# Key/query stores and weight loads in one order on SyncE in the first batched stage, and the third round's output weights behind the keys in the chain's first segment

## The chip, the cores and the metric

The kernel runs on one core of a Trainium2 chip. The metric is device time in microseconds (us) of one execution; a measurement is the median of several. A core has TensorE (PE in the profile; PEld is its weight loads), VectorE (DVE), ScalarE (ACT), GpSimd (POOL) and SyncE (SP). SyncE only issues transfers. ACT and POOL compute and issue transfers too, and each engine works through its own instructions in order, so an ACT instruction that waits to issue a transfer holds back all ACT work behind it. The transfers themselves are done by 16 DMA engines that all queues share.

## The reference

There are four layers, A B A B, on x of 2048 rows and 640 columns in bfloat16. The change touches the A layers only, a memory-augmented recurrent attention:

```python
for s in range(n_seg):                      # 64 segments of 32 rows
    h = concatenate([mem, xs])              # 8 memory rows + 32 rows of x (normalised)
    q, k, v = h @ Wq, h @ Wk, h @ Wv        # 640 -> 32 heads of 192
    p = softmax(mask(q @ k.T * scale))      # memory rows see all, others the past
    o = (p @ v) @ Wo                        # 6144 -> 640
    mem = o[:8]; outs.append(o[8:])
```

Segment s needs the memory rows that segment s-1 made, so the segments form a chain. A layer B (a linear attention with softmax features) follows each layer A and is the same in both kernels.

## The kernel before

**Two parts of a layer A.** Keys, queries and values of a row of x do not depend on the memory. The kernel uses this for the last 8 rows of every segment: a *batched stage* (`A_pre`) computes their keys, queries and values for all 64 segments ahead, as large matmuls, and stores them to DRAM (`kqb_d` for keys and queries, `vb_d` for values). The *chain* (`A_chain`) then goes segment by segment with the 8 memory rows and the first 24 rows, and fetches the stored 8 rows' keys, queries and values as it goes.

**Rounds.** The 32 heads are done in four rounds of 8. A round has 1536 columns of each of Wq, Wk and Wv, each in five pieces of 128 partitions by 1536 columns (384 KB), so a round has 15 pieces. In on-chip memory (one tile, `arena`) most pieces stay for the whole layer. The last three of the five pieces of each matrix are *slots* shared by rounds 0 and 3: they are loaded again whenever the other round is next (`load_slot`, L620). Pieces that stay are loaded by `load_matrix` (L626).

**The first batched stage** (layer 0, `x_raw` given) goes through eight *turns*: rounds 3, 2, 1, 0, and in each round two halves h of the segments. A turn does the keys and queries (12 column blocks each, L818, two blocks per PSUM bank) and then the values (L835). Each full PSUM bank is evicted alternately by DVE (L87) and ACT (L89); there are eight banks. After each eviction one step of a list of *tasks* runs: these normalise x row block by row block (load of `ln_x` by POOL, moments on DVE, deviation on ACT, store of `xn` by POOL). Keys and queries of a turn are gathered in one of two buffers `st`, which lie in the area that later holds the output weights of rounds 1 and 2 (`wo_mid`), and one transfer of 1536 KB stores them (L824). That store is issued by ACT. Values are stored by POOL (L843). All weight pieces of a turn are issued by SyncE where the turn begins in the program; as SyncE waits for no computation there, except before a slot is refilled, it runs ahead.

**Output weights.** Wo is used in rounds as well. Rounds 1 and 2 have areas of their own (`wo_mid`), rounds 0 and 3 share one (`wo_end`) and are read from a copy in DRAM, `wo_rows`, that `lay_out_wo` makes once, from DRAM to DRAM. `early_wo` loads the eight parts (320 KB each) whose place is free before the stage ends, `late_wo` the others, at the start of the chain.

**The chain's first segment** works in the order: queries and keys of round 0, its values, then rounds 1 to 3, each with its scores, its weighting and its share of the output (`wo_round`, L996). When round 0's slot pieces have been used they are refilled for round 3 (L620): queries, then keys, then values. The order of issue on SyncE is the order of the program text; the four late parts of the output weights of round 2 (`late_wo(2)`) stand between the refill of the queries' slots and that of the keys'.

**Semaphores of transfers.** The compiled program gives the transfers of SyncE and ACT together eight semaphores in turn. A transfer waits, before it is issued, until the transfer that last had its semaphore has landed.

The batched stage of layer 2 (no `x_raw`) keeps its stores on ACT; for the order of its SyncE instructions the same program text holds.

Of the kernel before, what the change touches and what calls it, by code (L numbers as in the profile page):

```python
# [8 lines left out]
P = 128  # L9
BF16 = mybir.dt.bfloat16  # L10
# [105 lines left out]
class Kernel:  # L116
# [465 lines left out]
    def layer_A(self, xn_dram, at_dram, li, x_raw=None):  # L582
        nc, tc = self.nc, self.tc
        KC, NSEG = self.KC, self.NSEG
        dram = self.dram
        NR = 4
        PW = 1536
        self.kqb_d = dram.tile([NSEG, P, NR, 192], BF16, name=f"kqb{li}")
        self.vb_d = dram.tile([NSEG, NR, 2, 8, 896], BF16, name=f"vb{li}")
        self.otb_d = dram.tile([NSEG, P, 384], BF16, name=f"otb{li}")  # L590
        wview = self.wview
        wov = self.A_Wo.rearrange("h d m -> (h d) m").rearrange("(c p) m -> p c m", p=P)
        low = self.view(0, LATE)
        at = LATE
        res, slot = {}, {}
        for r in (3, 2):
            for m in "KQV":
                for b in range(KC - (SLOTS[m] if r == 3 else 0)):
                    res[m, r, b] = low[:, len(res) * PW:len(res) * PW + PW]
        assert len(res) * PW * 2 == LATE  # L600
        for m, r, b in [(m, 0, b) for m in "KQV" for b in range(KC - SLOTS[m])] + \
                [(m, None, b) for m in "KQV" for b in range(KC - SLOTS[m], KC)] + [(m, 1, b) for m in "KQV" for b in range(KC)]:
            v = self.view(at, 2 * PW)
            at += 2 * PW
            if r is None:
                slot[m, b] = v
            else:
                res[m, r, b] = v
        holds = {}
        wo_mid = self.view(at, 24 * 1280)  # L610
        wo_end = self.view(at + 24 * 1280, 12 * 1280)
        assert at + 36 * 1280 == ARENA
        unread = set(res)

        def load_slot(m, r, b, whole=False):
            if holds.get((m, b)) != r:
                holds[m, b] = r
                w = PW if whole or m in "QV" else PW // 2
                for h in range(0, PW, w):
                    nc.sync.dma_start(out=slot[m, b][:, h:h + w], in_=wview[m][:, b, PW * r + h:PW * r + h + w])  # L620

        def load_matrix(m, r):
            for b in range(KC):
                if (m, r, b) in unread:
                    unread.remove((m, r, b))
                    nc.sync.dma_start(out=res[m, r, b], in_=wview[m][:, b, PW * r:PW * r + PW])  # L626
                elif (m, r, b) not in res:
                    load_slot(m, r, b, True)

        early = {(0, 4), (0, 5), (2, 4), (2, 5), (1, 0), (1, 1), (1, 2), (1, 3)}  # L630

        def load_wo(r, into=None, part=range(6)):
            t = into if into is not None else wo_end[:, :] if r in (0, 3) else wo_mid[:, 7680 * (r - 1):7680 * r]
            for k in part:
                tk = t[:, 1280 * k:1280 * k + 1280]
                if r in (0, 3):
                    self.last_load = nc.sync.dma_start(out=tk, in_=self.wo_rows[r // 3, :, 1280 * k:1280 * k + 1280])
                else:
                    nc.sync.dma_start(out=tk.rearrange("p (c m) -> p c m", m=640),
                                      in_=wov[:, 12 * r + 2 * k:12 * r + 2 * k + 2, :])  # L640

        def piece(m, r, b):
            assert (m, r, b) in res or holds[m, b] == r
            return res[m, r, b] if (m, r, b) in res else slot[m, b]

        def lay_out_wo():
            if li == 0:
                self.wo_rows = dram.tile([2, P, 7680], BF16, name="wo_rows")
                for i, r in enumerate((0, 3)):
                    (nc.sync if x_raw is not None else nc.scalar).dma_start(out=self.wo_rows[i].rearrange("p (c m) -> p c m", m=640),  # L650
                                        in_=wov[:, 12 * r:12 * r + 12, :])

        def early_wo():
            for r in (2, 0, 1):
                load_wo(r, part=[k for k in range(6) if (r, k) in early])

        def late_wo(r, part=range(6)):
            load_wo(r, part=[k for k in part if (r, k) not in early])

        self.A_pre(xn_dram, li, load_matrix, piece, wo_mid, wo_end, lay_out_wo, early_wo, x_raw)  # L660
        self.A_chain(xn_dram, at_dram, li, load_slot, piece, load_wo, late_wo, wo_mid, wo_end, low)
        self.post_args = at_dram, wo_mid, wo_end, low
# [6 lines left out]
    def A_pre(self, xn_dram, li, load_matrix, piece, wo_mid, wo_end, lay_out_wo, early_wo, x_raw):  # L669


        nc, tc, ev, KC, NSEG = self.nc, self.tc, self.ev, self.KC, self.NSEG
        NR = 4
        SH = min(NSEG, 32)
# [3 lines left out]
        NH = NSEG // SH  # L678
# [3 lines left out]
        with ExitStack() as es:  # L682
# [73 lines left out]
            def all_rows():  # L756
                rows = [slice(P * b, P * b + P) for b in range(self.NB)]
                t = in_turn([norm_tasks(lambda x, q=q: nc.gpsimd.dma_start(out=x[:], in_=x_raw[q, :]),
                                        lambda xn, q=q: nc.gpsimd.dma_start(out=xn_dram[q, :], in_=xn[:]))
                             for q in rows])  # L760
                return [f for i in range(0, len(t), 2) for f in (*t[i:i + 2], None)]
# [23 lines left out]
            for h, ri, r in steps:  # L785
# [10 lines left out]
                        if x_raw is not None:  # L796
                            busy(3)
                xBT = columns(h)
                if (h, ri) == ((NH - 1, 0) if x_raw is None else (NH - 1, 2)):
                    lay_out_wo()  # L800
                st = sts[turn % 2]
                turn += 1
                if x_raw is not None and h == 0 and ri == 1:
# [3 lines left out]
                        tasks += tails(h1)  # L807
                if x_raw is not None and (h, ri) == (NH - 1, 0):
                    tasks += all_rows()
                for mi, m in enumerate("KQ"):  # L810
                    load_matrix(m, r)
                    w = [piece(m, r, b) for b in range(KC)]
                    for c0 in range(0, 12, CB):
                        ps = ps_.tile([P, 512], F32, name="ps_pre", tag="bank")
                        for i in range(CB):
                            c = c0 + i
                            for b in range(KC):
                                nc.tensor.matmul(ps[:, T * i:T * i + T], lhsT=w[b][:, P * c:P * c + P], rhs=xBT[:, b, :],  # L818
                                                 start=(b == 0), stop=(b == KC - 1))
                        G, xi = c0 // 6, c0 % 6  # L820
                        so = st[:, :, 96 * mi:96 * mi + 96].rearrange("p s (i g t) -> p i g s t", g=2, t=8)
                        evict(out=so[:, xi:xi + CB, G],
                              in_=ps[:, :].rearrange("p (i t s) -> p i s t", i=CB, t=8))
                nc.scalar.dma_start(out=self.kqb_d[SH * h:SH * h + SH, :, r, :].rearrange("s p f -> p s f"), in_=st)  # L824
                load_matrix("V", r)
                if h == NH - 1 and ri == NR - 1:
                    early_wo()
                w = [piece("V", r, b) for b in range(KC)]
                for k in range(NT):
                    vt = vts[nv % 2]  # L830
# [18 lines left out]
    def A_chain(self, xn_dram, at_dram, li, load_slot, piece, load_wo, late_wo, wo_mid, wo_end, low):  # L849
        nc, tc, KC, NSEG = self.nc, self.tc, self.KC, self.NSEG  # L850
        scale = float(self.Dh) ** -0.5
        NR = 4
        with tc.tile_pool(name=f"A{li}_ch", reuse_waits="tile", bufs=1) as sp, \
# [79 lines left out]
            def to_rows(raw, m):  # L933
                if m == "K":
                    nc.vector.transpose(out=KT[:, :, 0:64], in_=raw[:, :].rearrange("p (c j) -> p c j", j=64))  # L935
                else:
                    rv = raw[:, :].rearrange("p (x i j) -> p x i j", i=3, j=64)
                    nc.vector.transpose(out=QT[:, :, 0:4:3, 0:64], in_=rv[:, :, 0:3:2, :])  # L938
                    nc.vector.transpose(out=QT[0:64, :, 1, 0:64], in_=rv[0:64, :, 1, :])
                    nc.vector.transpose(out=QT[64:P, :, 2, 0:64], in_=rv[64:P, :, 1, :])  # L940
# [109 lines left out]
            for s in range(NSEG):  # L1050
# [4 lines left out]
                def q_or_k(m, n):  # L1055
                    ps = pqp.tile([P, 512], F32, name="ps_qk", tag="qk")
                    project(hT, ps, m, n, s, range(KC))
                    return to_raw(ps, "OT" if m == "K" and n == 0 else "raw")
# [9 lines left out]

                to_rows(q_or_k("Q", 0), "Q")
                if s == 0:  # L1070
                    late_wo(2)
                    fill(FILL[li])
                to_rows(q_or_k("K", 0), "K")
                if s > 0:
                    store_rows(s - 1)
                pv = v_banks()
# [136 lines left out]
```

## Time and profile before

| | us |
|---|---|
| median of 3 runs | 3757.66 (3756.19 to 3761.43) |
| span of the profiled execution | 3763.4 |
| PE busy | 3553.2 (94%) |
| DVE busy | 2370.4 (63%) |
| ACT busy | 2074.7 (55%) |
| POOL busy | 1656.0 (44%) |
| first batched stage, first to last of its matmuls | 10.0 to 195.0 |
| first chain segment of layer 0 | 195.0 to 230.3 |
| second chain segment of layer 0 | 230.3 to 252.0 |
| first chain segment of layer 2 | 2065.1 to 2101.6 |

The transfers move 931.72 MB in the whole span. The stores of keys and queries are 1536 KB each, 16 in the two A layers, and take 8.9 us from issue to landing in the median, from 7.5 to 21.7. How to read it: busy time of an engine says little about what bounds a stage, because shares are averages over stages. Read the stretch of time in question, look for idle PE in it, and follow what ended each idle time.

### The profile page before, as it was taken

The page shows a single profiled execution, that of the slowest core. Times are in us where ns is not written, and L with a number is a line of the kernel's source. Part 1 is how long each engine was busy: PE and PEld are TensorE (multiplying, and loading weights), DVE is VectorE, ACT ScalarE, POOL GpSimd, SP SyncE. Part 2 cuts the span into 40 slices and gives each one's busy share as a digit, 9 for nine tenths or more (in the row PEclk, how much of TensorE's full clock was granted, in tenths as well). Part 3 has the DMA queues.
Part 4 walks back from the last instruction along what each step waited for, and adds up shares of the span by engine and source line. Part 5 has one row for each costly group of instructions (what it writes and reads, how often), then busy time and mean ns, then how long its engine had stood idle before and what let it go on. Part 6 is the DMA issues. An engine that isn't in the chain of part 4 may idle for free.

```text
span 3763.4 us, 169092 instructions
## 1 busy us (share of the span) xinstructions
PE 3553.2 (94%) x71082; PEld 2321.8 (62%) x71390; DVE 2370.4 (63%) x6330; ACT 2074.7 (55%) x5285; POOL 1656.0 (44%) x4323
## 2 busy tenths in 40 slices
PE   7989999999999999989899999999999999999898
PEld 5756666666666666555367566666666666665553
DVE  4556666666666666546633566666666666664565
ACT  2356566666666666546432556666666666665453
POOL 2445455555555555430342445555555555553400
PEclk9999999999999999989899999999999999999899
DMA  9788788888887878830387878888887888879100
GB/s 342 231 282 290 262 285 291 277 288 275 287 288 270 291 279 284 305 111 1 134 261 201 292 270 292 276 293 285 286 283 273 287 285 281 294 267 317 57 1 29
DMA packets 531381, 931.72 MB, mean 248 GB/s; under 512 B 141034, under 2 KB 298362, under 8 KB 530618
## 3 DMA queue, kind: packets, MB, share of 16 engines
q1 hardware_dynamic: 395898, 806.29, 60.9%
q0 software_dynamic: 68160, 88.78, 8.1%
q10 hardware_dynamic: 66560, 25.82, 2.7%
q8 instruction: 558, 9.14, 1.0%
q14 instruction: 205, 1.68, 0.1%
HBM read 852.43 MB, written 72.09 MB: 246 GB/s over the span
## 4 chain that ended last, share of the span: by engine, by line
PE 62%; DMA 13%; DVE 8%; ACT 6%; issue 5%; POOL 3%; PEld 2%; SPq 1%; POOLq 0%; ACTq 0%; DVEq 0%
PE ps_qk L920 19%; PE ps_w L996 8%; PE ps_v L920 8%; DMA arena<-wo_rows 6%; PE ps_o L970 4%; PE ps_s L962 4%; PE ps_pre L818 3%; PE ps_s L1028 2%; DVE hT L876 2%; PE ps_s L957 2%; DMA Vp<-vb 2%; PE ps_idle L1003 2%; PE ps_qk L389 2%; PE ps_pre L835 2%; DVE E L1035 1%
## 5 line engine op out<-in xcount | busy, mean ns | idle before, releaser
L920 PE MATMUL ps_qk<-arena,hT 128*32 128x384 bf16 x20480 | 999.1, 327 | 19.9 <-DMA arena<-in_A_Wk_dram 9.0
L920 PEld LDWEIGHTS <-hT 128*32 128x32 bf16 x30720 | 738.0, 96 | 437.0 <-DVE hT L1139 28.9
L930 ACT ACTIVATE raw<-ps_qk 128x384 bf16<-128x384 f32 x1024 | 502.9, 491 | 390.2 <-PE ps_s L1028 245.7
L996 PE MATMUL ps_w<-arena,OT 128*32 128x160 bf16 x24576 | 545.0, 235 | 36.8 <-issue 23.6
L903 POOL DMA_DIRECT2D Vp<-vb x512 | 258.8, 505 | 671.8 <-PE ps_o L970 462.6
L920 PE MATMUL ps_v<-arena,hT 128*32 128x384 bf16 x10240 | 537.2, 330 | 0.0
L996 PEld LDWEIGHTS <-OT 128*32 128x32 bf16 x24576 | 436.7, 97 | 132.2 <-issue 54.8
L935 DVE STREAM_TRANSPOSE KT<-raw 128x384 bf16<-128x384 bf16 x512 | 296.0, 578 | 205.7 <-ACT raw L930 201.7
L938 DVE STREAM_TRANSPOSE QT<-raw 128x256 bf16<-128x256 bf16 x512 | 227.9, 445 | 238.5 <-ACT raw L930 196.4
L891 POOL DMA_DIRECT2D kqb<-kqb x512 | 291.1, 568 | 163.0 <-POOL KT L899 148.2
L951 DVE CAST Vp<-ps_v 64x384 bf16<-64x384 f32 x512 | 286.0, 559 | 89.4 <-ACT Vp L949 75.8
L989 POOL DMA_DIRECT2D otb<-otb x512 | 282.8, 552 | 118.1 <-DVE otb L985 100.5
L949 ACT ACTIVATE Vp<-ps_v 64x384 bf16<-64x384 f32 x512 | 246.3, 481 | 149.6 <-PE ps_v L920 108.2
L976 DVE CAST OT<-ps_o 128x192 bf16<-128x192 f32 x512 | 183.2, 358 | 221.2 <-PE ps_o L970 203.2
L1035 DVE TENSOR_TENSOR E<-E,ps_s 80x320 bf16<-80x320 bf16 x512 | 247.4, 483 | 73.7 <-ACT ps_s L1034 69.7
L1014 ACT ACTIVATE E<-ps_s 80x320 bf16<-80x320 f32 x512 | 221.9, 433 | 127.7 <-PE ps_s L962 99.3
L970 PEld LDWEIGHTS <-Vp 80*128 80x128 bf16 x4096 | 183.8, 99 | 160.5 <-issue 124.8
L970 PE MATMUL ps_o<-E,Vp 80*128 80x80 bf16 x4096 | 234.2, 202 | 26.7 <-DVE E L1035 7.5
L962 PE MATMUL ps_s<-QT,KT 128*80 128x80 bf16 (+1 forms) x3072 | 233.7, 213 | 22.3 <-DVE KT L935 11.7
L975 ACT ACTIVATE OT<-ps_o 128x192 bf16<-128x192 f32 x512 | 167.8, 328 | 148.3 <-PE ps_o L970 147.1
L884 ACT ACTIVATE Vp<-ps_w 32x160 bf16<-32x160 f32 x512 | 150.7, 294 | 177.1 <-DVE wt L1138 151.5
L962 PEld LDWEIGHTS <-KT 128*80 128x80 bf16 x3072 | 195.6, 119 | 70.9 <-issue 59.8
(152 smaller groups left out, 5471.9 us busy)
## 6 DMA issues: line engine op xcount, KB each, us to landing
arena<-wo_rows SPq DMA_DIRECT2D x792, 320.0 KB, 6.9
arena<-in_A_Wq_dram SPq DMA_DIRECT2D x427, 384.0 KB, 4.6
arena<-in_A_Wv_dram SPq DMA_DIRECT2D x427, 384.0 KB, 6.3
arena<-in_A_Wk_dram SPq DMA_DIRECT2D x768, 192.0 KB, 4.8
kqb<-arena ACTq DMA_DIRECT2D x16, 1536.0 KB, 8.9
kqb<-kqb POOLq DMA_DIRECT2D x512, 48.0 KB, 5.1
arena<-in_A_Wk_dram SPq DMA_DIRECT2D x43, 384.0 KB, 6.4
vb<-arena POOLq DMA_DIRECT2D x128, 112.0 KB, 5.7
```

Source lines behind the costliest of these rows:

```text
L891: nc.gpsimd.dma_start(out=kqb[:], in_=self.kqb_d[s, :, r, :])
L903: nc.gpsimd.dma_start(out=Vs[n % 2][64:80, :], in_=self.vb_d[s, r].rearrange("g t f -> (g t) f"))
L920: nc.tensor.matmul(o[32 * g:32 * g + 32, 0:384], lhsT=hT[:, b, :], rhs=rhs, start=(i == 0), stop=(i == KC - 1), tile_position=(0, 32 * g), ...
L930: nc.scalar.activation(out=raw[:], in_=ps[:, 0:384], func=ACT.Copy)
L935: nc.vector.transpose(out=KT[:, :, 0:64], in_=raw[:, :].rearrange("p (c j) -> p c j", j=64))
L949: nc.scalar.activation(out=o, in_=i, func=ACT.Copy)
L951: nc.vector.tensor_copy(out=o, in_=i)
L962: nc.tensor.matmul(S[0:80, c0:c0 + 80 * (q1 - q0)], lhsT=KT[:, 3 * x + i, :], rhs=QT[:, x, q0:q1, :], start=False, stop=(x == 1 and i == 2 ...
L970: nc.tensor.matmul(O[x][:, 80 * i:80 * i + 80], lhsT=Vs[n % 2][0:80, 448 * x + k:448 * x + k + 128], rhs=E[0:80, 160 * x + 80 * e:160 * x ...
L989: nc.gpsimd.dma_start(out=self.otb_d[s, :, 96 * r:96 * r + 96], in_=otb[:, :, :].rearrange("p c t -> p (c t)"))
L996: nc.tensor.matmul(W[32 * g:32 * g + 32, 0:160], lhsT=OT[:, c, q:q + 32], rhs=w[:, 640 * i + 160 * g:640 * i + 160 * g + 160], start=(firs ...
L1035: nc.vector.tensor_tensor(out=E[0:80, 0:320], in0=E[0:80, 0:320], in1=rc, op=ALU.mult)
```

## The change

In the first batched stage the stores of keys and queries move from ACT to SyncE, into one order with the weight loads: a turn's store stands behind the round's values, and in the first half of a round the next round's 15 weight pieces follow the store directly. Before, the weights of a round were issued with no regard to stores. `lay_out_wo` now makes one of the two copies at a time, behind the stores of the second half of the rounds two and three, instead of both ahead of the second half of round three. `early_wo` is called ahead of the last turn's keys, where it was behind that turn's last weights. In the chain, `late_wo(2)` moves from ahead of the refill of the keys' slots to behind it; this holds for both A layers. The purpose is that no compute engine waits to issue a store, and that loads arrive in the order in which they are needed.

```diff
-        def lay_out_wo():
-            if li == 0:
-                self.wo_rows = dram.tile([2, P, 7680], BF16, name="wo_rows")
-                for i, r in enumerate((0, 3)):
-                    (nc.sync if x_raw is not None else nc.scalar).dma_start(out=self.wo_rows[i].rearrange("p (c m) -> p c m", m=640),
-                                        in_=wov[:, 12 * r:12 * r + 12, :])
+        if li == 0:
+            self.wo_rows = dram.tile([2, P, 7680], BF16, name="wo_rows")
+
+        def lay_out_wo(i):
+            nc.sync.dma_start(out=self.wo_rows[i].rearrange("p (c m) -> p c m", m=640), in_=wov[:, 36 * i:36 * i + 12, :])
...
-                if (h, ri) == ((NH - 1, 0) if x_raw is None else (NH - 1, 2)):
-                    lay_out_wo()
...
+                if x_raw is not None and h == NH - 1 and ri == NR - 1:
+                    early_wo()
                 for mi, m in enumerate("KQ"):
                     load_matrix(m, r)
...
-                nc.scalar.dma_start(out=self.kqb_d[SH * h:SH * h + SH, :, r, :].rearrange("s p f -> p s f"), in_=st)
                 load_matrix("V", r)
-                if h == NH - 1 and ri == NR - 1:
+                if x_raw is None and h == NH - 1 and ri == NR - 1:
                     early_wo()
+                stq = nc.scalar if x_raw is None else nc.sync
+                stq.dma_start(out=self.kqb_d[SH * h:SH * h + SH, :, r, :].rearrange("s p f -> p s f"), in_=st)
+                if x_raw is not None:
+                    if h == 0 and ri + 1 < NR:
+                        for m in "KQV":
+                            load_matrix(m, NR - 2 - ri)
+                    if h == NH - 1 and ri in (1, 2):
+                        lay_out_wo(ri - 1)
...
                 to_rows(q_or_k("Q", 0), "Q")
                 if s == 0:
-                    late_wo(2)
                     fill(FILL[li])
                 to_rows(q_or_k("K", 0), "K")
+                if s == 0:
+                    late_wo(2)
```

## The prediction

> **What bounds the kernel now.** I read busy time by stretch first, then the instructions in order of time, then who waited for whom. The first batched stage runs from 11.2 to 195.0 us. In stretches of 25 us (columns: length; PE, PEld, DVE, ACT, POOL busy with counts; granted clock; DMA share; GB/s):
>
> ```profile
> 25.00:50.00 25.00, 25.00 (x202) 19.16 (x200) 14.72 (x41) 7.78 (x18) 7.55 (x14) 1.00 0.98 333
> 50.00:75.00 25.00, 17.81 (x141) 14.24 (x139) 9.47 (x29) 6.12 (x16) 8.97 (x29) 0.86 1.02 378
> 75.00:100.00 25.00, 15.09 (x111) 11.36 (x109) 8.04 (x24) 4.08 (x11) 5.45 (x10) 0.86 0.99 329
> 100.00:125.00 25.00, 20.40 (x157) 15.46 (x154) 13.66 (x40) 6.16 (x18) 9.78 (x18) 0.93 1.02 335
> 125.00:150.00 25.00, 25.00 (x210) 20.26 (x208) 17.67 (x50) 9.61 (x22) 8.75 (x16) 1.00 0.58 168
> 150.00:175.00 25.00, 25.00 (x195) 18.92 (x194) 11.97 (x27) 7.41 (x15) 9.70 (x18) 1.00 0.61 162
> ```
>
> PE has holes from 50 to 125 us, while the DMA engines are full; from 125 on PE is full and the DMA engines are 40% empty. The holes, from PE in order of time (start, length, what, idle before and its releaser):
>
> ```profile
> 62.25 10.32 PE L818 MATMUL ps_pre<-arena 128*128 128x256 bf16 x80 [7.19 <-ACT arena L89]
> 81.68 2.34 PE L818 MATMUL ps_pre<-arena 128*128 128x256 bf16 x20 [1.52 <-DVE arena L87]
> 92.41 11.68 PE L818 MATMUL ps_pre<-arena 128*128 128x256 bf16 x90 [8.39 <-ACT arena L89]
> 110.31 6.33 PE L835 MATMUL ps_pre<-arena 128*128 128x384 bf16 x30 [4.60 <-DVE arena L87]
> ```
>
> PE waits for PSUM evictions, which stand still because ACT waits. What ACT waits for is in the waits (total us, times, longest):
>
> ```profile
> ACT arena L89 <- DMA arena<-in_A_Wk_dram: 17.3, 1, 17.3
> ACT arena L89 <- DMA arena<-in_A_Wq_dram: 14.7, 1, 14.7
> ```
>
> And in those of SyncE's queue (total, times, longest):
>
> ```profile
> SPq L626 <- DMA kqb<-arena: 26.4, 2, 14.4
> ```
>
> An eviction needs no weights. The instruction ahead of it on ACT is the store of L824: it issues at 61.12 and 91.30 us, just as those waits end. The built instruction lists say why: all DMAs of SyncE and ACT share eight semaphores in turn, so each waits until the one eight places before has landed. The second store's semaphore was last used by a query weight piece of round 1, the third's by a key piece of round 0, both weights wanted only later; SyncE in turn waits for the first store. The chain of work names the same path (start, length):
>
> ```profile
> 26.35 20.37 DMA kqb<-arena
> ...
> 52.52 8.51 DMA arena<-in_A_Wq_dram
> ...
> 79.55 11.65 DMA arena<-in_A_Wk_dram
> ...
> 96.17 11.94 DMA ln_x<-in_A_x_dram
> ```
>
> Then the chain's first segment: 195.0 to 230.3, 35.3 us, while the next takes 21.7 (230.31 to 251.97). PE waits there for late loads; layer 2 shows the same (2065.1 to 2101.6, 36.5 us):
>
> ```profile
> PE ps_qk L920 <- DMA arena<-in_A_Wk_dram: 4.2, 3, 2.8
> PE ps_w L996 <- DMA arena<-wo_rows: 2.8, 2, 1.6
> PE ps_qk L920 <- DMA arena<-in_A_Wq_dram: 1.0, 2, 0.9
> ```
>
> **What the Trainium skill says.** "DMA: Bandwidth & Descriptors", section "Issuing engines are not separate DMA queues": transfers from all queues run on the same 16 DMA engines. So moving stores from ACT to SyncE buys no bandwidth; it removes ACT's wait. The trace agrees: in stretches of 5 us with a share near 1.0 the sum is 280 to 400 GB/s whoever issues. Its "Queues, rings and completion order" says each DMA engine takes turns between queues; that fits a store that takes 20.37 us to land behind weights but 7.5 at best. "TensorE: Matmul & The Clock Gate", Part 1: an idle TensorE falls to half clock and needs some microseconds to return. The trace agrees: the granted clock is 0.50 at 60 to 65 and at 90 to 95 us.
>
> **The change, part by part.**
>
> *Stores to SyncE, weights one round ahead.* A turn of PE takes 19.6 us unhindered (136.08 to 155.68). Eight from 11.2, with 0.6 for the transposes in the first, end at 168.6 instead of 195.0: 26.4 us less. It is the four holes (21.7) plus slow matmuls behind three of them: 80 took 10.32 us and 90 took 11.68 where 120 take 13.1 elsewhere (+1.6 and +1.8), and 30 took 6.33 where 40 take 6.5 (+1.4). ACT also loses 8 issues of 0.37 us, at no gain, since it idles between evictions.
>
> The added wait: on SyncE a store waits for its turn's last evictions, and the next round's weights are queued behind it. First use against landing decides. DMA time by shares of the first 235 us: ACT's store queue 21.5%, so 6.3 us a store; weights 46.6% for 40.06 MB, so 16.1 us for a round of 5.9 MB (15 pieces of 384 KB), 5.4 for a copy of output weights (1920 KB), 7.2 for the eight early output pieces; POOL's queue 18.7% for 13.5 MB, so 3.0 a turn of value stores and 1.1 for each of 16 x rows in and out. In the new order:
> store 0 is ready at 26.4 (SyncE idles some 5 us first); store 0, round 2, values and five x rows end near 57, the first third of the weights near 42 (needed 50.5). Store 1 and values: 66. Store 2 is ready at 63.6; it and round 1, with values and x rows: 100, keys near 82 (needed 89.7), values needed 102.8. Store 3, first copy, store 4: 118. Round 0: 141 to 144, keys near 127 (needed 128.9), values needed 142. Store 5: 150, and its buffer is wanted again at 151. Second copy, store 6, early pieces: 172. Store 7: 178, values: 181.
> So every deadline holds, but from 118 on by 0 to 3 us only, and the stage ends with a DMA backlog: PE is done at 168.6, the last store lands some 10 us later; before it landed at 197.4, 2.4 after PE. The chain's output pieces wait for this store's buffer, and all slot weights are queued behind them. They come 5 to 8 us later against PE than before. I take 6 given back; both ends: 0 (my shares count time in which queues overlap; sums exceed 1.0) and 14 (V of round 0, store 5 and the chain each late by 3 to 8).
>
> *Early output pieces ahead of the last keys; copies moved.* Same loads, same order among themselves, waiting for buffers as before; their cost is in the sum above, and PE hides it. Zero.
>
> *Chain: round 2's output pieces behind the keys.* Four pieces of 320 KB leave the path of the six key pieces. At 377 GB/s (2080 to 2090) that is 3.5 us. In layer 2 the key waits sum to 4.7 and the values, whose place in the queue is unchanged, would land 1.18 MB behind the old last key (2090.2): 2091.3 to 2093.3, against use at 2090.3 onward after the shift. So about 3 of 3.5 remain. The moved pieces are used 5 us later still (2096.36): hidden. Ends: 1 (values then wait) and 5 (less slow clock, which was 0.52 from 2090 to 2100). I take 3 in each layer; in layer 0 it partly pays the backlog.
>
> *Sum:* 26.4 - 6 + 3 + 3 = 26.4 us; 3757.7 - 26.4 = 3731.
>
> **Rivals.**
> *PE alone bounds the stage:* nothing given back, and the chain gains 4 each: 3757.7 - 34.4 = 3723. For it: before moved weights up to 45 us earlier than needed, and, summed over stretches of 5 us, 32 us of DMA time lay idle up to 225. Against: those 32 us are just about what it would use up.
> *The DMA engines become the bound:* values of round 0 and store 5 are late, DVE waits for x rows (30.5 us before, longest 9.9) go on, and the chain starts on a backlog: 14 given back, no gain in layer 0's chain: 3757.7 - 26.4 + 14 - 2 = 3743; up to 3748. For it: the margins of 0 to 3 us. Against: with ACT's ring silent, x rows share the engines with one queue less.
> *Head of line, slower:* stores on SyncE take 20.4 us as store 0 did before, 14 more than assumed. One stands ahead of the keys of each later round, whose margins are 8, 8 and 2 us: 6 + 6 + 12 late; store 5, with 1 us of margin, adds 13: 37 lost against 26.4 won: 3768. Against: the 20.4 were spent sharing with weights that now stand behind the store.
>
> **How the numbers follow.** Forecast 0.50, PE alone 0.20, DMA bound 0.24, head of line 0.06. Range 3719 (chain ends at their best, 4 us under the second case) to 3748. Of the DMA-bound case a tenth falls within 0.2% (7.5 us). Faster 0.92, same 0.03, slower 0.05.
>
> **What would show it.** No wait of ACT for weights; PE without holes from 11 to 130 us and the stage's last L835 near 169; SyncE waiting for evictions, harmlessly; DMA share near 1.0 up to 180. Key waits gone in both chains, value waits small. It is wrong if PE waits for weight DMAs in the stage, if evictions wait for a store's landing, or if layer 0's first segment is longer than 35 us by more than about 6.

## The result and the profile after

| | before | after |
|---|---|---|
| median, us | 3756.93 (3755.62 to 3761.43, 4 runs) | 3736.57 (3723.82 to 3738.84, 4 runs) |
| ratio | | 0.9937, 95% interval 0.9913 to 0.9961 |
| span of the profiled execution, us | 3763.4 | 3735.3 |
| end of the first batched stage, us | 195.0 | 169.0 |
| first chain segment of layer 0, us | 35.3 | 40.1 |
| first chain segment of layer 2, us | 36.5 | 35.5 |

The change makes the kernel 0.5 to 0.6% faster: 20 us by the medians and 24 by the ratio (interval 15 to 33), where 26.4 were forecast (3731, range 3719 to 3748). The gain is in the first batched stage; the chain's first segment behind it gives part of it back.

After, in stretches of 25 us with the columns of before:

```profile
25.00:50.00 25.00, 24.77 (x200) 18.91 (x198) 12.99 (x34) 8.44 (x20) 6.55 (x13) 1.00 0.93 306
50.00:75.00 25.00, 25.00 (x208) 20.22 (x207) 16.06 (x49) 7.49 (x20) 15.27 (x41) 1.00 0.94 280
75.00:100.00 25.00, 25.00 (x212) 20.48 (x210) 17.93 (x52) 9.17 (x24) 10.04 (x19) 1.00 1.01 371
100.00:125.00 25.00, 25.00 (x206) 19.88 (x204) 15.43 (x44) 8.13 (x21) 9.31 (x17) 1.00 1.06 329
125.00:150.00 25.00, 24.75 (x194) 18.73 (x193) 12.05 (x28) 7.30 (x16) 9.30 (x17) 1.00 1.03 353
150.00:175.00 25.00, 23.95 (x255) 19.92 (x342) 8.65 (x16) 7.86 (x16) 9.41 (x20) 1.00 1.09 320
```

PE is full and at full clock where it had holes, and the DMA engines, which were 40% empty from 125 us on, are full to the stage's end. All that PE still waits for between 10 and 169 us (total us, times, longest):

```profile
PE ps_pre L817 <- DMA arena<-in_A_Wk_dram: 0.9, 2, 0.7
PE ps_pre L841 <- DVE arena L87: 0.2, 1, 0.2
```

The waits of ACT for weights are gone from its list; the waiting is now SyncE's:

```profile
SPq L827 <- DVE arena L87: 27.8, 4, 16.8
```

From 169 to 210 us PE waits for loads, as before, but for others and for longer:

```profile
PE ps_w L1002 <- DMA arena<-wo_rows: 8.4, 4, 5.5
PE ps_v L926 <- DMA arena<-in_A_Wv_dram: 3.3, 3, 2.1
PE ps_qk L926 <- issue: 1.1, 1, 1.1
PE ps_s L968 <- POOL KT L905: 0.8, 1, 0.8
PE ps_qk L926 <- DMA arena<-in_A_Wk_dram: 0.7, 1, 0.7
```

The keys, 4.2 us before, are down to 0.7. The output pieces that are read from `wo_rows` (rounds 0 and 3) went from 2.8 to 8.4, and 5.5 of it is the first piece of round 0. SyncE in order of time shows why (start, length of issue):

```profile
134.76 11.23 SPq L650 DMA_DIRECT2D wo_rows<-in_A_Wo_dram  x1
146.09 1.99 SPq L827 DMA_DIRECT2D kqb<-arena  x1
148.13 11.93 SPq L639 DMA_DIRECT2D arena<-in_A_Wo_dram  x2
160.16 1.70 SPq L637 DMA_DIRECT2D arena<-wo_rows  x2
162.59 1.93 SPq L639 DMA_DIRECT2D arena<-in_A_Wo_dram  x4
164.63 0.40 SPq L827 DMA_DIRECT2D kqb<-arena  x1
169.15 5.00 SPq L637 DMA_DIRECT2D arena<-wo_rows  x1
180.38 0.89 SPq L639 DMA_DIRECT2D arena<-in_A_Wo_dram  x2
181.63 1.68 SPq L637 DMA_DIRECT2D arena<-wo_rows  x3
```

The two pieces of L639 at 180.38 waited 6.2 us for the last store to land, whose buffer they take over. It was issued at 164.63 behind a queue of copy, store and early pieces and landed at 180.4: 11.3 us after PE had left the stage. Before, the same two pieces followed PE's last matmul of the stage (195.0) by 2.4 us:

```profile
197.40 0.99 SPq L639 DMA_DIRECT2D arena<-in_A_Wo_dram  x2
```

The three pieces behind them in the queue are those that PE wants.

### The profile page after: what moved, and what is told of

Its sections match the earlier page's. It is cut to its first block, busy times and chain, and to the rows that moved or that the text cites. A ratio compares the mean times of both kernels' runs of the same rounds, so it can differ in the third digit from the quotient of the medians.

```text
span 3735.3 us, 169098 instructions
## 1 busy us (share of the span) xinstructions
PE 3543.7 (95%) x71082; PEld 2319.9 (62%) x71390; DVE 2368.0 (63%) x6330; ACT 2073.4 (56%) x5285; POOL 1658.5 (44%) x4323
## 4 chain that ended last, share of the span: by engine, by line
PE 35%; DVE 5%; DMA 5%; ACT 4%; issue 4%; POOL 2%; PEld 2%; SPq 0%; POOLq 0%; DVEq 0%; ACTq 0%
PE ps_qk L926 9%; PE ps_w L1002 4%; PE ps_v L926 4%; PE ps_o L976 2%; PE ps_s L968 2%; PE ps_qk L389 2%; DMA arena<-wo_rows 2%; PE ps_pre L817 1%; PE ps_s L1034 1%; DVE hT L882 1%; PEld L817 1%; PE ps_s L963 1%; PE ps_idle L1009 1%; PE ps_v L419 1%; PE kv L429 1%
```

## The experiments

The theory: ACT stood at its stores because they shared semaphores with weight loads that ran ahead; with one order on SyncE it doesn't, PE bounds the stage, and the DMA work that used to be done beside idle time comes due at its end. The rivals: it was the order of the other loads that helped, or the landing of the stores; loading one round ahead is not needed; the longer first segment has nothing to do with a backlog. Times alone can't tell small steps apart here: 47 runs of the kernel before on one chip spread from 3748.54 to 3773.83. So I read stage ends and segment lengths in traces, and give times beside. Each kernel has one trace, the changed one two, so a difference of 1 us between two traces says little.

**ACT issues the stores again.** Only this is undone:

```diff
-                stq = nc.scalar if x_raw is None else nc.sync
+                stq = nc.scalar
```

> The changed kernel with the first stage's stores issued by ACT again; weights, copies, early pieces and the chain's order stay as changed. Theory A (the gain is that ACT no longer waits, through the shared semaphores, for a weight load before it may issue a store): the holes of PE return, waits of ACT for weight loads of 14 to 17 us show again, the stage ends at 185 to 200 us instead of 169. Theory B (the gain is the order of copies and early pieces, or the chain): the stage ends at 169 to 175.

Measured: 3759.16 us, ratio to before 0.9998 (0.9983 to 1.0013). The stage ends at 191.7. The holes are back: PE's waits in the stage, where before had 15.6 us in two, and what ACT waited for:

```profile
PE ps_pre L817 <- ACT arena L89: 16.4, 2, 9.8
ACT arena L89 <- DMA arena<-in_A_Wq_dram: 32.7, 2, 19.5
```

Two stores held ACT up for 32.7 us, for landings of query weights. All the rest of the change was in this kernel, and its stage ends where that of the kernel before ends in a second trace (191.7, below), so the rest alone wins nothing in the stage, and the move of the stores is what makes it work.

**GpSimd issues the stores** of the kernel before, whose transfers have semaphores of their own; weights run ahead as before:

```diff
-                nc.scalar.dma_start(out=self.kqb_d[...], in_=st)
+                (nc.scalar if x_raw is None else nc.gpsimd).dma_start(out=self.kqb_d[...], in_=st)
```

> The kernel before, with only the first stage's stores issued by GpSimd's queue, whose semaphores are its own; weights still run ahead of everything. Theory A: no wait of ACT for weights, at most small holes; the stage ends at 169 to 178 us. Theory B' (the stores land late because weights stand in front of them on the shared DMA engines, and the two key/query buffers are then not free for evictions): holes of 5 us or more stay, now as evictions that wait for the landing of a store, and the stage ends at 185 or later.

Measured: 3753.35 us, ratio 0.9989 (0.998 to 0.9998). PE's last matmul of the stage ends at 181.7, between the two expectations. PE's waits from 10 to 197 us:

```profile
PE ps_qk L920 <- DVE hT L876: 13.9, 1, 13.9
PE ps_pre L835 <- DVE arena L87: 6.7, 2, 4.5
PE ps_pre L818 <- DVE arena L87: 4.4, 4, 1.6
```

and what held DVE and ACT up in the stage:

```profile
DVE ln_stats L221 <- DMA ln_x<-in_A_x_dram: 46.8, 12, 11.4
ACT arena L89 <- DMA arena<-in_A_Wq_dram: 4.1, 1, 4.1
```

ACT's wait for weights is down to 4.1 us, and with it go the two large holes, without any new order of the loads. So ACT's wait at its stores was the larger cause. That it waited through shared semaphores is seen in the trace of the kernel before, which notes the semaphore of every transfer: SyncE and ACT use the same eight, GpSimd eight others. The store issued at 61.12 has the semaphore of a query piece that landed at 61.03, and the one at 91.30 that of a key piece that landed at 91.20. What stays, 11 us of PE, is DVE waiting for x rows, which GpSimd issues too. In part its semaphores now tie them to the stores: it waited for stores ahead of x loads 9.6 us and ahead of value stores 21.9 us, and DVE's longest wait, 11.4 us, is for an x row issued behind such a wait. Two others, of 7.0 and 6.9 us, are for x rows that took 9.2 and 9.6 us to land; why they took so long is open. The first segment's rows came late on the same queue (13.9 us); the late output pieces arrived meanwhile, and the segment took only 24.5 us after it. A queue on which something else is due is no place for the stores either.

**No loading ahead.** The changed kernel without:

```diff
-                    if h == 0 and ri + 1 < NR:
-                        for m in "KQV":
-                            load_matrix(m, NR - 2 - ri)
```

> The changed kernel without the loads one round ahead: stores on SyncE, but a round's weights are issued only when their own round comes up on SyncE, that is behind the store of the round before. Worked out: the keys' first piece is issued when the second half's store is ready, 6.5 us before PE needs it, behind the store's 6.3 us of DMA time and with about 2 us of latency: PE waits 5 to 10 us in each of three rounds, with slow clock behind, and the stage ends at 185 to 205 us, with PE waiting for weight DMAs. If loading ahead were idle ornament, the stage would end at 169 to 173.

Measured: 3786.14 us, ratio 1.0071 (1.0045 to 1.0097). The stage ends at 223.1, later than I had worked out. PE's waits in it:

```profile
PE ps_pre L817 <- DMA arena<-in_A_Wk_dram: 43.6, 15, 13.8
```

The first of the three later rounds waits 6.7 us for its first key piece, as expected; the next two 13.5 and 13.8, where a copy of output weights stands ahead of the keys as well, which I had left out of the sum. With the stores in the order of the loads and no round of loads behind them that nobody wants yet, the stage ends 54 us later than in the changed kernel, and the kernel 28 us slower than before. This is the wait that the rival "head of line" names, made to happen, though not by its cause: the six stores whose landing the trace has took 8 to 10 us here, not 20.

**The chain's move alone,** in the kernel before:

```diff
-                    late_wo(2)
                     fill(FILL[li])
                 to_rows(q_or_k("K", 0), "K")
+                if s == 0:
+                    late_wo(2)
```

> The kernel before, with only the chain's move of round 2's output pieces behind the keys. Predicted: each first segment 3 us shorter (35.3 to 32.3 in layer 0, 36.5 to 33.5 in layer 2), 6 us in all. From the changed kernel's trace, where the values' slot pieces then were waited for by 2.8 and 0.5 us in layer 2: 1 us in each, so a time 0 to 3 us below before's.

Measured: 3760.78 us, ratio 1.0 (0.9989 to 1.0011). The stage, which this edit doesn't touch, ends at 191.7. Segments of 34.6 us in layer 0 and 34.6 in layer 2, so 0.8 and 1.9 less than before. Three of PE's waits in layer 0's:

```profile
PE ps_qk L920 <- DMA arena<-in_A_Wk_dram: 2.4, 2, 1.7
PE ps_w L996 <- DMA arena<-wo_rows: 2.3, 3, 1.6
PE ps_v L920 <- DMA arena<-in_A_Wv_dram: 1.5, 2, 0.9
```

The keys still wait 2.4 of 4.2 us, and the values, which did not wait before, now do.

**The chain's move undone,** in the changed kernel (the same lines the other way):

> The changed kernel with round 2's output pieces ahead of the keys again in both chains. By the prediction (3 us in each layer) the first segments grow from 40.1 to 43 us in layer 0 and from 35.5 to 38.5 in layer 2; by the run with that move alone (0.8 and 1.9 us), to 41 and to 36.3. The stage ends at 169 in both cases, and the time is at most a few us above the changed kernel's.

Measured: 3739.72 us, ratio 0.9956 (0.9937 to 0.9974). 39.1 us in layer 0, so not longer than with the move (40.1, and 39.9 in a second trace); 36.7 in layer 2. In layer 0 PE waits for keys, 0.7 us with the move,

```profile
PE ps_qk L926 <- DMA arena<-in_A_Wk_dram: 4.8, 3, 3.4
```

but not for values, and less for output pieces (5.5 us instead of 8.4). The last store also landed 1 to 3 us sooner after the stage's end than in the two traces with the move, so layer 0 doesn't show the move by itself here. Taking the traces of layer 2 whose round 2 pieces stand directly behind the keys or, in the old order, ahead of them: 36.5, 36.1, 36.7 with the old order, 35.5, 34.0, 32.8, 34.2, 34.6, 33.1, 34.5 with the new. (The run with two more places changed on SyncE, 35.6, is left out.) The move is worth about 2 us there (36.4 less 34.1). In layer 0 without a backlog three traces with the move took 34.6, 34.6 and 35.5 us, and the one without it 35.3: 0 to 1.

**The copies in the holes.** In the changed kernel the two copies stand behind the last stores of rounds 2 and 1, the second and third in the stage's order. The DMA engines stood at 0.44 of their share from 20 to 30 us and at 0.69 from 60 to 70, while SyncE waited for evictions. The copies go there:

```diff
+                if x_raw is not None and (h, ri) == (0, 0):
+                    lay_out_wo(0)
                 stq = nc.scalar if x_raw is None else nc.sync
...
-                    if h == NH - 1 and ri in (1, 2):
-                        lay_out_wo(ri - 1)
+                    if (h, ri) == (NH - 1, 0):
+                        lay_out_wo(1)
```

> The changed kernel with the two copies of output weights moved from behind the stores of the second and third round to two places where the DMA engines were half idle: the first behind the first round's values ahead of the first store (share 0.32 and 0.56 at 20 to 30 us), the second behind the first round's second store (share 0.73 and 0.65 at 60 to 70). Theory of the backlog: the last store, which landed at 180.4, lands 5 to 9 us earlier, the output pieces that wait for its buffer too, and layer 0's first segment shrinks from 40.1 to 32 to 35 us; 5 to 8 us off the time. Rival (the backlog is not what the first segment waits for: its loads are bound by the value stores or by their own number): 39 to 40 us. A second rival: the first copy delays the first store and round 2's weights, and PE waits in the stage.

Measured: 3737.07 us, ratio 0.9941 (0.9923 to 0.9959). The share from 20 to 30 and 60 to 70 rises to 0.83 and 1.05. The first segment takes 35.7 us instead of 40; PE's wait for output pieces in it, 8.4 us in the changed kernel:

```profile
PE ps_w L1004 <- DMA arena<-wo_rows: 3.3, 3, 1.6
```

The second rival did not come true: PE's only wait in the stage after its start is 0.3 us. Its first matmuls began late (12.5 us) and ran at half clock (0.51 from 10 to 15 us), which put the stage's end at 171.7. The last store was to land 5 to 9 us before 180.4 and landed at 177.9, later than in the second trace of the changed kernel (177.0). It came 6.2 us after the stage's end instead of 11.3 and 9.1, but in good part because the stage ended later; the segment itself ended at 207.4, against 209.1 and 207.8. So this trace alone does not show that the backlog shrank. The two further runs with the copies in these places do: their stages ended at 170.2 and 169.7, and the last store landed at 173.8 and 172.0.

**And round 2's pieces behind the values' slots:**

```diff
                 v_rows(pv, 0)
+                if s == 0:
+                    late_wo(2)
```

> As the run with the copies in the holes, and round 2's output pieces one place further back, behind the refill of the values' slots. If the values' wait in the chain (2.8 and 0.5 us in layer 2, 2.1, 0.3 and 0.9 in layer 0) is the move's own price, it goes: 1 to 3 us off each first segment; if these pieces are then wanted before they land, PE waits at the output of round 2 instead, and the length stays.

Measured: 3741.13 us, ratio 0.9957 (0.9942 to 0.9973). 34.1 us in layer 0, 35.0 in layer 2. The two pieces behind the last store follow the stage's end by 3.6 us:

```profile
173.83 1.30 SPq L639 DMA_DIRECT2D arena<-in_A_Wo_dram  x2
```

The values no longer wait, but PE now waits at round 2's output (0.6 and 0.6 us) and for the round 3 pieces behind: no gain of this step is shown. In the stage PE waited once for a query piece of round 0, 1.6 us, so the copies in these places are not quite free.

**One more copy** of the same size, into a scratch tensor nobody reads:

```diff
                         lay_out_wo(ri - 1)
+                    if h == NH - 1 and ri == 2:
+                        scratch = self.dram.tile([P, 7680], BF16, name="wo_scratch")
+                        nc.sync.dma_start(out=scratch[:]..., in_=...[:, 12:24, :])
```

> The changed kernel with one more copy of 1920 KB, from DRAM to a scratch tensor nobody reads, behind the second of its two copies. It adds nothing that PE waits for by data, only 5.4 us of DMA time ahead of the last two stores. Theory of the backlog: the last store lands some 5 us later and layer 0's first segment grows from 40.1 to 43 to 46 us; perhaps the stage also ends later, as evictions then wait for a store. Rival (the DMA engines have slack there): 40 us.

Measured: 3737.49 us, ratio 0.9949 (0.993 to 0.9968). The stage ends at 169.3, the first segment takes 43.9 us, and the two pieces behind the last store are issued at 184.0:

```profile
170.22 0.40 SPq L827 DMA_DIRECT2D kqb<-arena  x1
170.72 9.38 SPq L637 DMA_DIRECT2D arena<-wo_rows  x1
184.02 0.89 SPq L639 DMA_DIRECT2D arena<-in_A_Wo_dram  x2
```

So 5.4 us of DMA time more (by the prediction's estimate for a copy), and the segment 4 us longer.

**Two more places changed on SyncE,** on top of the copies in the holes: `early_wo` for round 2 ahead of the seventh store, `late_wo(1)` behind `late_wo(0, range(3))`.

> As the run with the copies in the holes, and two more places changed on SyncE: the early output pieces of round 2 (which wait for nothing) go ahead of the wait for the seventh store's evictions, where the DMA engines stood at 0.5 to 0.7 of their share, and the two late pieces of round 1, which wait for the last store, go behind the three late pieces of round 0, which PE wants first. If PE's first wait in the chain is for SyncE standing at the last store, it goes (1.3 and 1.6 us) and layer 0's first segment shrinks from 35.7 to 32 to 34 us; if those pieces wait for the value stores' buffers anyway, it stays at 34 to 36. In time 0 to 4 us below the run with the copies in the holes, 6 to 10 below the changed kernel.

Measured: 3743.17 us, ratio 0.995 (0.9931 to 0.9969), 35.4 us in layer 0. Waits for output pieces of round 0 fell to 0.8 and 0.5 us, but the slot pieces of queries, 1.8, 1.3 and 0.6, and of values took their place. 10.6 MB move in these 35 us; shortening one wait moved it to the next piece in the queue. The 6 to 10 us expected below the changed kernel did not come: the changed kernel beside it, next, has the same time.

**The changed kernel again,** beside the last:

> The changed kernel as it is, on the same chip as its further variant, for its time beside it and for a second trace: the stage ends at 169 to 172, layer 0's first segment takes 39 to 41 us, layer 2's 33 to 36; the time is 17 to 26 us below before's.

Measured: 3742.07 us, ratio 0.9949 (0.9933 to 0.9965), 20.0 us below before on this chip. The stage ends at 167.9; 39.9 us and 34.0 us.

Across these runs the length of layer 0's first segment can be set against the time from the stage's end to the issue of the pieces behind the last store. Two runs are left out: with GpSimd's stores the segment began late for another reason, and with two more places changed these pieces stand elsewhere.

| kernel | lag, us | first segment, us |
|---|---|---|
| no loading ahead | 2.3 | 35.5 |
| ACT issues the stores again | 2.4 | 34.6 |
| chain's move alone | 2.4 | 34.6 |
| before | 2.4 | 35.3 |
| copies in holes, late behind values | 3.6 | 34.1 |
| copies in holes | 6.2 | 35.7 |
| chain's move undone | 8.2 | 39.1 |
| changed, second trace | 9.1 | 39.9 |
| changed | 11.3 | 40.1 |
| one more copy | 14.7 | 43.9 |

Up to a lag of 6 us the segment takes 34 to 36 us whatever the lag; beyond that it grows by about as much as the lag.

No version with the copies in the holes is told from the changed kernel in time. In the traces the second chain segment begins at 204 to 207 us instead of 208 to 209, at most 5 us or 0.13%, which is less than the uncertainty of any of these times.

## Why the prediction was right, and where its sizes were off

*What bounded the stage.* Right, and shown from both sides: with ACT issuing, the holes stand although everything else is changed; with another issuer they shrink although nothing else is. The semaphores of the two held stores and the landings at 61.03 and 91.20 say what ACT waited for.

*The stage, "26.4 us less".* The end was put at 168.6 and came at 169.0 and 167.9. The size hangs on the other end: the two further kernels with ACT's stores, one of them with the stage of before untouched, both ended their stage at 191.7. The execution I read had a hole of 4.60 us for x rows, which was 1.44 us in the one with the stage of before and 0.23 in the other. So the stage won 26 us against that trace and 23 against these: 3 us of my sum were chance of one execution.

*Deadlines.* All held, in the order given: keys of round 0, with a margin of 2 us, waited 0.25; values of round 0 and store 5, with 0 to 3, did not hold PE up. The last store was put at 178 and landed at 180.4 and 177.0. The waits of DVE for x rows went on (36.2 us against 30.5; longest 7.1 against 9.9), but PE's waits for DVE's evictions came to 0.2 us instead of 6.1. DMA time summed from shares of the profile was thus good to some 3 us over 170.

*"6 given back".* The segment grew by 4.8 us with the move in it; without it the changed kernel's grew by 3.8 against before. So 4 to 5 instead of 6: about right. That it is the backlog is shown by one more copy, which made the segment 4 us longer. With both copies moved out of the stage's end it was 4 to 6 shorter (35.7, 34.1 and 35.4), which agrees, though the first of these stages ended late and the other two runs have a further change of order each.

*"Zero" for the early output pieces and the copies.* Neither was tried by itself behind SyncE's stores. With ACT's stores they won nothing in the stage. The copies were counted in the sum of DMA time, but their place is not free: it is part of the backlog just named.

*"I take 3 in each layer".* This is the term that was mis-sized: 0 to 1 and about 2 us instead of 3 and 3. I counted the keys' 3.5 us and let the values wait only a little; they took 1.5 us of it in layer 0 without a backlog and 3.2 in layer 2 after. As I read it, where several pieces of one queue arrive one behind the other and each is wanted soon after the one before, a change of order mostly moves the wait to another piece.

*The rate of the DMA engines.* One reading was too tidy. I wrote that stretches of 5 us with a share near 1.0 move 280 to 400 GB/s whoever issues. In the kernel before, from 155 to 160 us the share is 1.03 and the rate 262, and from 175 to 180 it is 0.99 and 225; a store of keys and queries was under way in both. The stage's sum used DMA time by queue and not this rate.

*The sum.* 23 to 26 less 4 to 5, plus 2 in layer 2, is 20 to 24; measured 20.4 by the medians (24 by the ratio, 9 of uncertainty either way) and 20.0 in the second measurement. The range of 29 us also held the numbers of "PE alone" (3723) and "DMA bound" (3743, a gain of 14), and the times hardly rule out the second, since the second measurement's interval begins at a gain of 13. The traces decide: "PE alone" failed by the backlog, and "DMA bound" by its mechanism, as nothing in the stage was late by more than 0.25 us.

## What to carry to other kernels

When an engine that computes also issues transfers, look at what its issue instruction waits for, not only at what it moves: a store can wait for a load that has nothing to do with it, and hold up an engine that is 55% busy until PE runs dry. Moving it to a queue that computes nothing is safe only if the loads behind it are wanted later than the store's wait lasts; count the deadlines one by one, and fill the wait with transfers whose time doesn't matter. Work that used to be done ahead in idle DMA time comes due somewhere: look at the stage behind for what it costs there.

## What the runs showed of the hardware

A transfer issued on SyncE straight behind a store of keys and queries takes long to issue, though it waits for no semaphore. A store is 4096 packets of 384 bytes. In the changed kernel:

```profile
26.26 0.38 SPq L827 DMA_DIRECT2D kqb<-arena  x1
26.69 4.81 SPq L626 DMA_DIRECT2D arena<-in_A_Wk_dram  x1
...
91.51 12.31 SPq L650 DMA_DIRECT2D wo_rows<-in_A_Wo_dram  x1
```

and with the copies in the holes, where the first copy stands behind weights and the second behind a store:

```profile
18.60 0.69 SPq L650 DMA_DIRECT2D wo_rows<-in_A_Wo_dram  x1
...
51.24 10.44 SPq L650 DMA_DIRECT2D wo_rows<-in_A_Wo_dram  x1
```

A copy of the same size issues in 0.69 us or in 10.44, and the DMA engines were as busy at the first (share 1.05 from 15 to 20 us) as at the second (1.03 from 50 to 55). On SyncE such waits cost PE little: in the stage of the changed kernel no wait of PE for a weight exceeds 0.7 us. An engine that computes stands still for it: with ACT issuing the stores again, the fourth store took 6.32 us to issue, 15 us behind the third, which had not landed. A store is not the only transfer with this effect. With GpSimd's stores, none of which is in SyncE's queue, the second of two copies, which move rows of 1280 bytes, took 12.44 us to issue right behind the first, which took 0.69. (A store of GpSimd's was under way then too; an earlier one, at 25.77, did not slow SyncE's weight pieces, which took 0.33 us each.) That the queue has no room left behind the many packets of a store or a copy is my reading; it was not tried with a smaller store.
